# Linear attention on one core: how the rows of five output stores are cut into DMA transfers

## Chip, core and metric

The kernel runs on one core of a Trainium2 chip. The metric is the device time of one execution in microseconds (us); lower is better. Times are the median of several runs; 168.23 us is the median before (3 runs, 168.01 to 168.49).

## What is computed

Linear attention with an ELU feature map, for 32 heads, 2048 positions and 128 features, in bf16:

```python
B, H, S, D = 1, 32, 2048, 128          # q, k, v: bf16 [B, H, S, D]

def reference(q, k, v):
    phi_q = jnp.where(q > 0, q + 1, jnp.exp(q)) + 1e-6
    phi_k = jnp.where(k > 0, k + 1, jnp.exp(k)) + 1e-6
    kv = jnp.einsum("bhsd,bhse->bhde", phi_k, v)
    z = jnp.einsum("bhsd->bhd", phi_k)
    num = jnp.einsum("bhqd,bhde->bhqe", phi_q, kv)
    den = jnp.einsum("bhqd,bhd->bhq", phi_q, z)[..., None] + 1e-6
    return num / den
```

Each head reads three matrices of 512 KB and writes one.

## The kernel before

The work goes head by head, 32 in all. The 2048 positions of a head lie as 128 partitions of 16 positions each, so that one partition holds 16 x 128 bf16 values, a contiguous piece of 4 KB in DRAM. A load or a store of a whole head is therefore 128 rows of 4 KB.

For one head the steps are: ScalarE takes exp of k (line 368); VectorE clips it (line 382); GpSimd makes the positive part (line 372) and adds the two for some tiles (line 390); TensorE multiplies phi_k with v, and with a column of ones for z, into one PSUM bank (lines 413 and 320); ScalarE copies that to SBUF (line 430). TensorE transposes q into PSUM (line 436), ScalarE and VectorE make the parts of phi_q from it (lines 447, 454, 456, 468), and TensorE multiplies them with the copied state (lines 483 and 484). VectorE takes the denominators (506), their reciprocals (512), and divides into `o_sb` (517 and 524). For the last two heads ScalarE does some of the divisions (536).

k, q and v have 6 buffers each, the output has 10 (`NBO`): head h stores from buffer h % 10, and head h+10 may write there once that store has landed.

The order on each engine is written out by a small planner. Every operation is added with an engine and a number, its key; each engine runs its operations in the order of the keys, and the planner puts in the semaphore waits that follow from what operations read and write. All loads and stores are issued by the SP engine, one after the other: a load at line 361, with keys h - 7.95 (k), h - 6.9 (q) and h - 6.8 (v), and a store at line 571, with the key `late = h + 1.0 + 0.18 * h` (line 575). So stores fall further and further behind their heads: the loads of head 31 have keys of about 24, so the stores of heads 20 to 31 are all issued after the last load, in the order of the heads. Within a head's store the pieces have one key and are issued in the order in which they are added.

`PARTS` (line 252) says for which heads the store is cut, and into how many partitions each piece has; other heads are stored in one transfer of 128 partitions (lines 577 to 580). All pieces of a store count on the same semaphore. Head 31 is stored in two transfers of all 128 partitions, the first 9 of the 16 positions of each (rows of 2304 bytes) and the other 7 (1792 bytes); it isn't touched. Before, `PARTS` cuts head 29 alone.

Of the kernel before, what the change touches and what calls it, by code (L numbers as in the profile page):

```python
# [231 lines left out]
def bass_standalone__linear_attn_elu__prompt_kernel(  # L232
# [16 lines left out]
    NG = 7  # L249
    HALF = NT * P // 2  # L250
    LAST = NH - 1
    PARTS = {LAST - 2: (51, 13, 64)}

    ADD = (10, 11, 12, 13, 14)
    EVEN, ODD = tuple(range(0, NT, 2)), tuple(range(1, NT, 2))
# [9 lines left out]
    with ExitStack() as es:  # L265
# [85 lines left out]
        for h in range(NH):  # L351
# [218 lines left out]
            def store(t0, t1, key, parts, slot, p0=0, p1=P, h=h, bo=bo):  # L570
                pl.add("sp", key, lambda sp: sp.dma_start(rows(of, h)[p0:p1, t0 * D:t1 * D],
                                                          o_sb[p0:p1, bo, t0:t1].rearrange("p j d -> p (j d)")),
                       reads=[("o", bo, p) for p in parts], dma=("o", slot))

            late = h + 1.0 + 0.18 * h
            if h < LAST:
                p0 = 0
                for n in PARTS.get(h, (P,)):
                    store(0, NT, late, ("t", 0, 1, 2, 3, 4), bo, p0, p0 + n)
# [35 lines left out]
```

## Time and profile before

| | |
|---|---|
| median of 3 runs | 168.23 us (168.01 to 168.49) |
| the profiled execution | 167.82 us |
| its span, first to last instruction | 166.5 us |
| granted TensorE clock | 0.997 |
| busy: PE, DVE, ACT, POOL | 94%, 91%, 93%, 64% of the span |
| HBM read, written | 50.33 MB, 16.78 MB: 403 GB/s over the span |
| loads and whole stores, from issue to landing | 15.0 to 15.3 us |
| first store issued (line 571), last store issued | 20.9 us, 162.9 us |

The profile is one execution. "Busy" is an engine's time in instructions as a share of the span. A DMA transfer is split over the core's 16 DMA engines. The trace has a record for each packet that an engine moved (here a row of 4 KB, and a closing packet of 4 bytes that counts the semaphore up), with start and duration but without the number of the engine, and an event for each landing on a semaphore. The page lists the transfers of the stores by size; the whole ones are one line, the pieces of heads 29 and 31 have a line each:

```profile
out_dram<-o_sb SPq DMA_DIRECT2D x30, 512.0 KB, 15.3
out_dram<-o_sb SPq DMA_DIRECT2D x1, 288.0 KB, 3.7
out_dram<-o_sb SPq DMA_DIRECT2D x1, 256.0 KB
out_dram<-o_sb SPq DMA_DIRECT2D x1, 224.0 KB, 3.6
out_dram<-o_sb SPq DMA_DIRECT2D x1, 204.0 KB
out_dram<-o_sb SPq DMA_DIRECT2D x1, 52.0 KB
```

Columns are what is moved, the queue, the operation and its count, the size of one, and the median us from issue to landing where the trace has it: 51, 13 and 64 rows of 4 KB are 204, 52 and 256 KB.

### The profile page before, as it was taken

The numbers are of one execution on the slowest core, as the hardware profiler recorded it, in microseconds if no ns is written. First come the engines' busy times: TensorE is split into PE (matmuls) and PEld (weight loads), VectorE is DVE, ScalarE is ACT, GpSimd is POOL, SyncE is SP. The second block draws the span as 40 slices with busy tenths as digits, with TensorE's granted clock in tenths as the row PEclk, the third lists the DMA queues.
The fourth block names the chain that finished last, engine by engine and source line by source line (L and its number), as shares of the span: only waits on it lengthen the run. The fifth ranks groups of instructions, "written<-read, shape, count | busy, mean of one in ns | idle before, by whom it ended". The sixth has DMA issues, their size and how long they took to land.

```text
span 166.5 us, 6269 instructions
## 1 busy us (share of the span) xinstructions
PE 156.0 (94%) x2819; PEld 145.3 (87%) x2453; DVE 152.3 (91%) x270; ACT 155.0 (93%) x143; POOL 106.3 (64%) x128
## 2 busy tenths in 40 slices
PE   7789999999999999999999999999999999999960
PEld 0259999999999999899999989999998999999950
DVE  0587999999999999999999999999999999999991
ACT  3979999999999999999999999999999999998790
POOL 2405788676767877676778867676787767677300
PEclk9999999999999999999999999999999999999998
DMA  5999999999999999999999999999999999999986
GB/s 205 345 417 421 413 415 419 412 407 418 417 416 419 422 417 417 422 421 411 424 420 414 423 421 415 419 421 415 422 420 416 422 421 418 418 421 418 415 310 239
DMA packets 18605, 67.25 MB, mean 404 GB/s; under 512 B 2082, under 2 KB 2210, under 8 KB 18594
## 3 DMA queue, kind: packets, MB, share of 16 engines
q1 hardware_dynamic: 18592, 67.12, 99.4%
q8 instruction: 5, 0.08, 0.2%
q14 instruction: 6, 0.05, 0.1%
q10 hardware_dynamic: 2, 0.00, 0.0%
HBM read 50.33 MB, written 16.78 MB: 403 GB/s over the span
## 4 chain that ended last, share of the span: by engine, by line
DVE 58%; PE 17%; POOL 12%; ACT 6%; issue 3%; DMA 2%; DVEq 0%
DVE o_sb L524 20%; POOL rk_sb L390 12%; DVE rq_sb L456 11%; DVE emk_sb L382 10%; DVE emq_sb L468 9%; PE kvz_ps L413 6%; PE o_ps L483 5%; PE o_ps L484 5%; ACT ek_sb L368 3%; DVE rden_sb L512 3%; DVE o_sb L517 3%; ACT eq_sb L447 2%; DMA k_sb<-in_k_dram 2%; DVE den_sb L506 2%; DVE rk_sb L390 1%
## 5 line engine op out<-in xcount | busy, mean ns | idle before, releaser
L413 PE MATMUL kvz_ps<-v_sb,rk_sb 128*128 128x129 bf16 (+1 forms) x512 | 67.0, 220 | 2.8 <-DVE rk_sb L390 1.0
L524 DVE TENSOR_TENSOR o_sb<-o_ps,rden_sb 128x768 bf16<-128x768 f32 (+2 forms) x62 | 67.8, 1135 | 0.0
L390 POOL TENSOR_TENSOR rk_sb<-rk_sb,emk_sb 128x640 bf16<-128x640 bf16 x30 | 41.9, 1395 | 39.5 <-DVE emq_sb L468 38.2
L372 POOL TENSOR_SCALAR rk_sb<-k_sb 128x1024 bf16<-128x1024 bf16 (+1 forms) x60 | 64.1, 1068 | 2.5 <-DMA k_sb<-in_k_dram 2.5
L483 PE MATMUL o_ps<-kvs_sb,emq_sb 128*128 128x129 bf16 (+1 forms) x536 | 65.2, 217 | 0.0
L484 PE MATMUL o_ps<-kvs_sb,rq_sb 128*128 128x129 bf16 (+1 forms) x536 | 64.4, 217 | 0.0
L368 ACT ACTIVATE ek_sb<-k_sb 128x2048 bf16<-128x2048 bf16 x32 | 61.0, 1907 | 2.6 <-DMA k_sb<-in_k_dram 2.6
L447 ACT ACTIVATE eq_sb<-xT_ps 128x2048 bf16<-128x2048 bf16 (+1 forms) x33 | 60.0, 1821 | 2.0 <-PE xT_ps L436 2.0
L413 PE MATMUL kvz_ps<-v_sb,emk_sb 128*128 128x129 bf16 (+1 forms) x338 | 53.3, 221 | 0.6 <-DVE emk_sb L382 0.3
L413 PEld LDWEIGHTS kvz_ps<-v_sb,rk_sb 128*128 128x128 bf16 x512 | 46.1, 98 | 7.6 <-POOL rk_sb L390 2.7
L483 PEld LDWEIGHTS o_ps<-kvs_sb,emq_sb 128*128 128x128 bf16 x536 | 51.2, 98 | 0.8 <-issue 0.3
L484 PEld LDWEIGHTS o_ps<-kvs_sb,rq_sb 128*128 128x128 bf16 x536 | 51.3, 98 | 0.0
L436 PE MATMUL xT_ps<-ident,q_sb 128*128 128x128 bf16 x512 | 33.8, 219 | 0.6 <-DMA q_sb<-in_q_dram 0.4
L436 PEld LDWEIGHTS xT_ps<-ident,q_sb 128*128 128x128 bf16 x512 | 29.9, 98 | 5.1 <-DMA q_sb<-in_q_dram 4.2
L413 PEld LDWEIGHTS kvz_ps<-v_sb,emk_sb 128*128 128x128 bf16 x338 | 32.5, 98 | 0.9 <-DVE emk_sb L382 0.5
L320 PE MATMUL kvz_ps<-ones_sb,rk_sb 128*128 128x1 bf16 x232 | 31.3, 165 | 0.0
L454 ACT ACTIVATE rq_sb<-xT_ps 128x1024 bf16<-128x1024 bf16 x30 | 30.9, 1029 | 0.0
L382 DVE TENSOR_SCALAR emk_sb<-ek_sb 128x2048 bf16<-128x2048 bf16 x32 | 22.0, 688 | 5.6 <-ACT ek_sb L368 5.6
L456 DVE TENSOR_SCALAR rq_sb<-xT_ps 128x1024 bf16<-128x1024 bf16 x34 | 23.3, 690 | 1.1 <-PE o_ps L484 1.0
L468 DVE TENSOR_SCALAR emq_sb<-eq_sb 128x2048 bf16<-128x2048 bf16 x32 | 22.1, 690 | 0.0
L320 PE MATMUL kvz_ps<-ones_sb,emk_sb 128*128 128x1 bf16 x121 | 19.9, 166 | 0.0
L430 ACT ACTIVATE kvs_sb<-kvz_ps 128x129 bf16<-128x129 f32 x32 | 9.0, 281 | 1.6 <-PE kvz_ps L413 0.9
(28 smaller groups left out, 49.2 us busy)
## 6 DMA issues: line engine op xcount, KB each, us to landing
k_sb<-in_k_dram SPq DMA_DIRECT2D x32, 512.0 KB, 15.0
q_sb<-in_q_dram SPq DMA_DIRECT2D x32, 512.0 KB, 15.1
v_sb<-in_v_dram SPq DMA_DIRECT2D x32, 512.0 KB, 15.1
out_dram<-o_sb SPq DMA_DIRECT2D x30, 512.0 KB, 15.3
out_dram<-o_sb SPq DMA_DIRECT2D x1, 288.0 KB, 3.7
out_dram<-o_sb SPq DMA_DIRECT2D x1, 256.0 KB
out_dram<-o_sb SPq DMA_DIRECT2D x1, 224.0 KB, 3.6
out_dram<-o_sb SPq DMA_DIRECT2D x1, 204.0 KB
```

The costliest lines, as they stand in the source:

```text
L320: return pe.add_instruction(mybir.InstMatmult(start_tensor_calc=start, stop_tensor_calc=stop, ldweights=False, bass_skip_group_check=True, ...
L368: lambda a, bi=bi, b2=b2: a.activation(ek_sb[:, b2, :], k_sb[:, bi, :], ACT.Exp),
L372: pl.add(eng, key, lambda e: e.tensor_scalar(rk_sb[:, b3, c], k_sb[:, bi, c], BIG, 0.0, op0=ALU.min, op1=ALU.max), reads=[("k", bi)] + ([( ...
L382: lambda d, b2=b2, b3=b3: d.tensor_scalar(emk_sb[:, b3, :], ek_sb[:, b2, :], 1.0, EPS, op0=ALU.min, op1=ALU.add),
L390: return e.tensor_tensor(out=a, in0=a, in1=b, op=ALU.add)
L413: last = pe.matmul(kvz_ps[:, 1 - l:NC], lhsT=w, rhs=v_sb[:, bi, c - l:c + D], start=first, stop=fin, skip_group_check=True)
L436: last = pe.transpose(xT_ps[:, j * P:(j + 1) * P], q_sb[:, bi, j * P:(j + 1) * P], ident[:])
L447: halves[part] = pl.add("act", key, lambda a: a.activation(eq_sb[:, b2, c], xT_ps[:, c], ACT.Exp), reads=both[part:part + 1] or both, writ ...
L456: f = lambda d: d.tensor_scalar(rq_sb[:, b3, c], xT_ps[:, c], 0.0, None, op0=ALU.max)
L483: pe.matmul(o_ap, lhsT=emq_sb[:, b3, t * P:(t + 1) * P], rhs=kvs_sb[:, b3, c0:c1], start=True, stop=False)
L484: return pe.matmul(o_ap, lhsT=rq_sb[:, b3, t * P:(t + 1) * P], rhs=kvs_sb[:, b3, c0:c1], start=False, stop=True)
L524: pl.add("dve", key, lambda d: d.tensor_tensor(out=o_sb[:, bo, 3 * g0:3 * g1, :].rearrange("p (a b) d -> p a b d", b=3), in0=_ap(full, bas ...
```

## The change

Heads 6, 12, 18 and 24 are stored as five transfers each, of 112, 4, 4, 4 and 4 partitions, and head 29 in one transfer of 128. Everything else stays: the keys, the buffers, the order of the heads, the bytes that are moved in all.

```diff
@@ -249,7 +249,7 @@
     NG = 7
     HALF = NT * P // 2
     LAST = NH - 1
-    PARTS = {LAST - 2: (51, 13, 64)}
+    PARTS = {h: (112, 4, 4, 4, 4) for h in (6, 12, 18, 24)}
 
     ADD = (10, 11, 12, 13, 14)
     EVEN, ODD = tuple(range(0, NT, 2)), tuple(range(1, NT, 2))
```

## The prediction

> **What bounds the kernel now.** I read the page's slices and DMA rows first, then a table of stretches, then the waits, then the trace's single DMA records.
>
> ```profile
> DMA  5999999999999999999999999999999999999986
> GB/s 205 345 417 421 413 415 419 412 407 418 417 416 419 422 417 417 422 421 411 424 420 414 423 421 415 419 421 415 422 420 416 422 421 418 418 421 418 415 310 239
> ...
> q1 hardware_dynamic: 18592, 67.12, 99.4%
> ```
>
> One slice is 166.5 / 40 = 4.16 us. From the second slice to the last but two, the 16 DMA engines are full, at some 418 GB/s; only the last two slices (310, 239) are not. The stretches say the same about the end:
>
> ```profile
> core 0: us, PE busy (x) PEld busy (x) DVE busy (x) ACT busy (x) POOL busy (x), PEclk, DMA share, GB/s
> 60.00:140.00 80.00, 78.86 (x1480) 76.35 (x1293) 78.42 (x133) 79.02 (x68) 57.74 (x68) 1.00 1.03 419
> ...
> 162.00:164.00 2.00, 0.00 (x0) 0.00 (x0) 0.84 (x3) 0.73 (x3) 0.00 (x0) 1.00 0.99 380
> 164.00:165.00 1.00, 0.00 (x0) 0.00 (x0) 0.00 (x0) 0.00 (x0) 0.00 (x0) 1.00 0.70 276
> 165.00:166.50 1.50, 0.00 (x0) 0.00 (x0) 0.00 (x0) 0.00 (x0) 0.00 (x0) 0.69 0.17 66
> ```
>
> VectorE, ScalarE and TensorE are as full as the DMA engines until 158 us, but after 164 none of them works: only DMA engines do, and fewer and fewer of them (0.70, then 0.17). So the last 1.5 us belong to a few DMA engines that are behind. The waits show that loads are not what compute waits for:
>
> ```profile
> PEld xT_ps L436 <- DMA q_sb<-in_q_dram: 4.2, 1, 4.2
> ACT ek_sb L368 <- DMA k_sb<-in_k_dram: 2.6, 2, 1.5
> POOL rk_sb L372 <- DMA k_sb<-in_k_dram: 2.5, 1, 2.5
> PE xT_ps L436 <- DMA q_sb<-in_q_dram: 0.4, 1, 0.4
> ```
>
> These few are from the first heads. Later there is room: v of head 28 has landed at 138.01 while that head's transposes, which run ahead of its use, start at 139.83.
>
> **Which engines are behind.** A whole store leaves 16 landing events, one per engine. Head 28's, the last store that this change leaves alone, come at 159.06 plus 0.00 0.00 0.12 0.22 0.23 0.31 0.32 0.37 | 1.39 1.45 1.72 2.20 2.22 2.52 2.63 4.02 us. Eight engines are ahead, eight behind. The lags stay from transfer to transfer, since every engine always has work: nothing absorbs them. They grow where an engine fetches code (rows of 16 KB, 0.94 to 0.98 us each, at 16.2, 23.3, 30.7 and 37.6 us, after each of which one lag is about 1.45 larger), and on one engine, the last, by about 0.13 in every store, whose 4 KB packets take 178 to 182 ns there in place of 159.
>
> Head 29's three pieces tell who is who. They leave 3+1, 13+1 and 16 landings (the +1 are early, at 157.64 and 158.05, for the engines not used): 51 rows run on 3 engines (17 each), 13 on 13 (one each), 64 on 16 (four each). The two engines that run 17 rows after head 28 and can be followed from packet to packet are those with lags 1.39 and 1.45; the engine with 4.02 runs one row and then four, so it is in numbers 3 to 12. So are those with 1.72, 2.52 and one of 2.20 and 2.22; the other of that pair runs four rows only (13 to 15). 2.63 is most likely in 3 to 12 too, which makes five of these ten behind and five ahead.
>
> The Trainium skill, page DMA: Bandwidth & Descriptors, section "Why a DMA increments its semaphore by 16 and not by 1", says that a transfer runs on the largest number up to 16 that divides its partition count, on the lowest-numbered engines. The counts 3, 13 and 16 agree; that they are the lowest-numbered no run here shows, but I call the three engines 0 to 2.
>
> **Price of a row.** A 4 KB packet takes 159 ns and the next starts 3.5 ns before its end: 155.5 ns. The closing 4-byte packet takes 9, net 5.5. A whole transfer is 8 x 155.5 + 5.5 = 1.25 us per engine, as its ends show (1248 to 1249 ns apart).
>
> **The change part by part.**
>
> Removed: head 29's three pieces. Engines 0 to 2 had 17+1+4 = 22 rows there, 3 to 12 had 5, 13 to 15 had 4; now each has 8. That is 14 rows and 2 closings fewer on 0 to 2 (14 x 0.1555 + 0.01 = 2.19 us), 3 more on 3 to 12 (0.47), 4 more on 13 to 15 (0.62).
>
> Added: in each of heads 6, 12, 18 and 24, 112 rows are 7 per engine, and four pieces of 4 rows give, by the same reading, one row each to engines 0 to 3. Engines 0 to 3 get 3 rows and 4 closings more per head, in all 12 x 0.1555 + 16 x 0.0055 = 1.95 us; 4 to 15 get 4 rows fewer (0.62).
>
> So a handicap at head 29's end is the lag of head 28 plus what the pieces add. Before: engines 0 and 1 have 1.39 and 1.45 + 2.19 = 3.58 and 3.64; the last one 4.02 - 0.47 = 3.55. These three are the ones that end the span: their packets go on without a gap through heads 30 and 31 (1.25 + 0.72 + 0.57 us) to the last landing at 166.48. After: 3.34 and 3.40 for 0 and 1, 4.02 - 0.62 = 3.40 for the last. Alone that is 3.64 - 3.40 = 0.24 us less.
>
> Engine 3 decides. It had 3 rows fewer and now has 12 more. If it is one of the five ahead, it ends at 0.37 + 1.95 = 2.32: harmless. If it is behind: 1.72 gives 3.67 (+0.03 against 3.64), 2.20 gives 4.15 (+0.51), 2.52 gives 4.47 (+0.83), 2.63 gives 4.58 (+0.94), 4.02 gives 5.97 (+2.33). The trace names no engine number. Its neighbours speak for behind: of 0 to 2 two of three are, of 13 to 15 one of three. I take the middle of the four that cost, +0.88 us.
>
> Hidden: SP issues 16 transfers more and 2 fewer. An issue at L571 takes 0.315 to 1.05 us when it isn't held up, so four more are 1.3 to 4.2 us of SP's time per head, and the k, q and v loads behind them on its queue wait so long. Cover: loads take 15.0 us from issue to landing, so the engines have more than ten us of queue. Without that cover it would be up to 4.2 us per head.
>
> Hidden too: the loads on engines 0 to 3 land later, by 0.98 us after head 12's store (6 rows, 8 closings) and 1.47 after head 18's, against 1.8 us or more of room (138.01 to 139.83, and 150.66 to 153.98 for head 31's v). Their waits take the place of nothing.
>
> Unknown: what a 4-row transfer costs beyond its row. Lower end 0 (the 13-row piece took 161 ns per busy engine, row and closing); upper end 0.28 us, as the first rows after an idle engine took 300 to 440 ns, so 16 x 0.28 = 4.5 us. I take 0, since these engines are never idle; that is the row it is nearest to. A saving is unknown as well: 28 rows of the slow engine in stores of 112 rows could run at 159 in place of 179 (0 to 0.56 us less).
>
> The Trainium skill, same page, section "Latency and other measured facts", says that DMA engines 7 and 15 are usually slower, and ties that to a kind of transfer not used here. Were the slow engine 7, engine 3 would not be it, and the +2.33 would fall out: the sum would then be the middle of three, +0.83. No run here shows its number.
>
> **Sum.** The profiled execution took 167.82, 1.3 around its span of 166.5. 167.82 + 0.88 = 168.70; the median of the runs is 0.41 above that execution, so 169.1.
>
> **Rivals.**
> - Engine 3 is ahead (or the 1.72 one): -0.24 to +0.03, so 168.0 to 168.3. For it: five of ten are ahead. Against it: its neighbours.
> - Faster: rows lie on engines otherwise than I read. If the 4-row pieces hit engines that are ahead and the slow engine's 28 rows in 112-row stores run at 159 ns, the handicaps are 0.83 on 0 and 1 and 4.02 - 0.62 - 0.56 = 2.84 on the slow one: 0.80 less, 167.4. It decides once no engine is above 3.1. Against it: the 3 and 13 fit the divisor reading.
> - The change doesn't do what it says: 4 rows are spread so that nobody gets more. Then 4.02 is left uncorrected, +0.38: 168.6. The 13-row piece on 13 engines speaks against it.
> - Small transfers cost a slow first row: 1 to 4.5 us more on engines 0 to 3, 169 to 172.7. Only idle engines show such rows.
>
> **Chances.** Forecast 0.51, engine 3 ahead 0.25, faster 0.15, spread 0.05, slow small rows 0.04. No change is within 0.3%, 0.5 us, about what can be told here. Slower: 0.51 + 0.04 + 0.01 of spread = 0.56. Same: 0.25 + 0.04 = 0.29. Faster: 0.15. The likeliest case alone reaches from +0.5 to +2.33, 168.7 to 170.6. Over all I give 167.6 to 170.6, which leaves out most of the faster case and the slow rows.
>
> **What would show it.** Right: each 4-row piece leaves 4 landings and one early one; one engine's lag grows by about 0.49 in each of the four cut stores from a start of 2 or more; head 28's largest lag is above 4.1; and after 165 us a single engine works on. Wrong: head 28's largest lag at 3.4 and a span of 166.2 to 166.5 (engine 3 ahead), 4-row pieces that leave other than 4 landings, or compute waiting for k, q or v after head 4.

## The result and the profile after

| | before | after |
|---|---|---|
| median (7 runs each) | 168.05 us (167.84 to 168.49) | 169.28 us (168.53 to 170.25) |
| ratio to before | 1 | 1.0076, 95% interval 1.0053 to 1.0099 |
| the profiled execution | 167.82 us | 170.25 us |
| its span | 166.5 us | 169.0 us |

The change makes the kernel slower, by 1.23 us in the medians. The profiled execution of after is the slowest of its seven runs, so its 2.43 us over that of before are more than the usual loss.

The page of after, its rows of slices and of DMA queues (one slice is 169.0 / 40 = 4.22 us):

```profile
DMA  5999999999999999999999999999999999999961
GB/s 198 350 416 421 415 415 419 414 422 413 417 419 420 419 417 420 415 420 420 421 419 419 419 421 416 420 418 419 421 419 419 418 422 420 418 420 415 379 279 69
...
q1 hardware_dynamic: 18640, 67.12, 98.0%
q8 instruction: 5, 0.08, 0.2%
q14 instruction: 6, 0.05, 0.1%
```

The middle is what it was, some 419 GB/s. The loss lies in the last slices: 69 GB/s in the last one, where before still had 239. The 48 packets more on q1 (18640 against 18592) are closing packets, 64 more in the four cut heads and 16 fewer in head 29; they cost no bandwidth that can be seen. Stretches of after, with the DMA share and GB/s in the last two columns:

```profile
core 0: us, PE busy (x) PEld busy (x) DVE busy (x) ACT busy (x) POOL busy (x), PEclk, DMA share, GB/s
60.00:140.00 80.00, 78.86 (x1479) 76.34 (x1290) 78.45 (x133) 79.04 (x69) 58.04 (x68) 1.00 1.03 419
...
162.00:164.00 2.00, 0.00 (x0) 0.00 (x0) 1.12 (x4) 0.98 (x4) 0.00 (x0) 1.00 0.97 388
164.00:165.00 1.00, 0.00 (x0) 0.00 (x0) 0.00 (x0) 0.00 (x0) 0.00 (x0) 1.00 0.62 244
165.00:166.50 1.50, 0.00 (x0) 0.00 (x0) 0.00 (x0) 0.00 (x0) 0.00 (x0) 0.57 0.23 91
166.50:169.00 2.50, 0.00 (x0) 0.00 (x0) 0.00 (x0) 0.00 (x0) 0.00 (x0) 0.50 0.05 20
```

Between 60 and 140 us all is equal to before. From 166.5 us on, where before had ended, 0.05 of 16 engines work: 0.8 of an engine, so one engine alone moves the last 2.5 us. Compute has no part in it, and the loads that now land later are not waited for; the waits of after list the same four as before, within 0.2 us:

```profile
PEld xT_ps L436 <- DMA q_sb<-in_q_dram: 4.3, 1, 4.3
...
ACT ek_sb L368 <- DMA k_sb<-in_k_dram: 2.8, 2, 1.6
...
POOL rk_sb L372 <- DMA k_sb<-in_k_dram: 2.6, 1, 2.6
...
PE xT_ps L436 <- DMA q_sb<-in_q_dram: 0.5, 1, 0.5
```

The landings of head 28's store in after, the first at 158.62 us, and then the lag of each engine behind it:

```
0.00 0.04 0.05 0.08 0.17 0.18 | 1.03 1.46 1.51 1.55 2.30 2.55 3.00 3.20 4.00 6.60
```

The engine that loses 0.13 us per store has its 4.00, as before (4.02). The other one, 6.60, is new, and it ends the kernel: head 31's last transfer has its first landing at 165.53, fifteen engines have landed by 166.43, and the last one lands at 168.92. In what follows this engine is called L.

### The profile page after: what moved, and what is told of

The parts are those of the page before. It is cut to its first block, busy times and chain, and to the rows that moved or that the text cites. A ratio compares the mean times of both kernels' runs of the same rounds, so it can differ in the third digit from the quotient of the medians.

```text
span 169.0 us, 6283 instructions
## 1 busy us (share of the span) xinstructions
PE 156.1 (92%) x2819; PEld 145.3 (86%) x2453; DVE 152.5 (90%) x270; ACT 155.2 (92%) x143; POOL 106.4 (63%) x128
## 3 DMA queue, kind: packets, MB, share of 16 engines
q1 hardware_dynamic: 18640, 67.12, 98.0%
## 4 chain that ended last, share of the span: by engine, by line
DVE 60%; PE 16%; POOL 12%; DMA 4%; issue 3%; ACT 1%; SPq 1%; DVEq 0%
DVE o_sb L524 21%; POOL rk_sb L390 12%; DVE rq_sb L456 11%; DVE emq_sb L468 10%; DVE emk_sb L382 10%; PE kvz_ps L413 5%; PE o_ps L483 5%; PE o_ps L484 5%; DMA k_sb<-in_k_dram 4%; DVE rden_sb L512 3%; DVE o_sb L517 3%; DVE den_sb L506 2%; ACT ek_sb L368 1%; SPq L361 1%; DVE rk_sb L390 0%
```

## Experiments

Every kernel is the one before with `PARTS` (line 252) changed, unless the diff shows more. e1 to e4 share one set of runs of before (median 168.08 us), e5 to e8 a second (167.96), e9 and e10 a third (167.91), e11 and e12 a fourth (167.95).

**e1_whole: no store is cut.**

```diff
-    PARTS = {LAST - 2: (51, 13, 64)}
+    PARTS = {}
```

> No store is cut but head 31's. Theory (an engine that is behind sets the end): the handicap of the slow engine stays at 4.02 and that of the engine with 2.63, which may also serve the code fetch near 158.5 us, at 2.63 to 4.08, against 3.64 before: 0.4 us slower than before, ratio 1.002 to 1.004, and 0.6 to 1.0 us faster than the changed kernel. Rival (small transfers or their issue cost the time): nothing small is left, so not slower than before, 1.000 or below.

Measured: 168.29 us, ratio 1.0008 (0.9986 to 1.0030). In head 28's store the largest lags are 2.43, 2.77 and 4.12: without a cut, the slow engine is last. The ratio expected was 1.002 to 1.004; the measured one can't be told from 1. Leaving the cut of head 29 out costs at most 0.3% of the time, 0.5 us; it isn't what costs 1.2 us, the four new cuts are.

**e2_three: which engines a piece runs on.**

```diff
-    PARTS = {LAST - 2: (51, 13, 64)}
+    PARTS = {h: (112, 3, 3, 3, 7) for h in (6, 12, 18, 24)}
```

> Heads 6, 12, 18 and 24 as 112, 3, 3, 3 and 7 partitions: five transfers each as in the changed kernel, with the same 11 rows on engines 0 to 2, but 8 in place of 11 on engine 3, and 8 in place of 7 on engines 4 to 6. Theory (engine 3 is the one that is late): 12 rows, 1.9 us, come off it, so the end is set by others at handicaps of 3.4 to 4.1: 168.0 to 168.5, ratio 1.000 to 1.003. Rival (small transfers or issue cost): as the changed kernel, 1.007. Second rival (the late one is among 0 to 2): as the changed kernel, 1.007.

Measured: 168.23 us, ratio 1.0008 (0.9990 to 1.0026). Across head 24's cut three lags grow by 0.65 us (1.96, 2.37, 2.52 to 2.61, 3.03, 3.15), three by 0.16 (2.06, 2.10, 2.15 to 2.20, 2.26, 2.32), and the slow engine's from 3.82 to 4.27, that is by its own 0.13 for each of two stores and 0.19 more. Three rows on each of three engines and one on four others is what pieces of 3 and 7 give when each runs on as many engines as it has rows, and the 3 are not among the other four. L, known here by its jump at 104 us (0.89 to 1.84, see e5), gains 0.16 in a cut, and at least 0.6 in every cut of after. So it is among the four engines of a 4-row piece, but not among the three of a 3-row piece: by the prediction's numbering it is engine 3. The slow engine is one of the next three (4 to 6).

**e3_even: five transfers, but the same rows on every engine.**

```diff
-    PARTS = {LAST - 2: (51, 13, 64)}
+    PARTS = {h: (64, 16, 16, 16, 16) for h in (6, 12, 18, 24)}
```

> Heads 6, 12, 18 and 24 as 64 and four times 16 partitions: five transfers each, all on 16 engines, so every engine has its 8 rows. Theory (imbalance): as with no cut at all, 0.4 us slower than before, 1.002 to 1.004. Rival (small transfers or issue cost): as the changed kernel or slower, 1.007 or more, since the four 16-partition pieces burden all 16 engines.

Measured: 168.46 us, ratio 1.0012 (0.9996 to 1.0027), span 167.1. Cutting four heads into five transfers each costs some 0.4 us at most (0.38 by the medians, 0.45 by the upper end of the interval). With e2, which also has five transfers a head, it shows that the number of transfers isn't what costs: the uneven rows do, where they fall on L.

**e4_who: pieces of n and 16 - n rows.**

```diff
-    PARTS = {LAST - 2: (51, 13, 64)}
+    PARTS = {h: (h - 7, 23 - h, 112) for h in range(8, 16)}
```

> Heads 8 to 15 as n, 16 - n and 112 partitions with n = 1 to 8, which gives engine j one row more for j < n and one more for j < 16 - n: a number for each lag in the landings. Theory: the engine with number 3 has a lag of 1.7 or more before head 8's store, and two of 0, 1 and 2 have less than that. Rival: engine 3 is one of the eight that are ahead. It also shows if 0 to n - 1 are the engines of a transfer of n rows: each cut should move the lags of n engines by 0.16 us. The time means little; 168 to 170.

Measured: one run of 169.15 us. Each of the eight cut stores leaves 34 landings, (n + 1) + (16 - n + 1) + 16, so each count up to 15 runs on just as many engines. A number for each of the 16 lags couldn't be had from it: several engines run within 0.1 us of each other and change places. For the numbering it is inconclusive.

The Trainium skill, page DMA: Bandwidth & Descriptors, section "Why a DMA increments its semaphore by 16 and not by 1", has the rule that these counts follow, the largest divisor up to 16, on the lowest-numbered engines. The runs bear out the count (34 landings here, 36 in a cut store of after), and that smaller sets lie within larger ones; the numbers themselves no record shows.

**e5_again: after, a second time**, with nothing changed from it.

> The changed kernel once more, for a second profile. Theory (engine 3, with a lag of about 1.7 of its own, gets 2.6 more than its neighbours by the four cuts; what code fetches add on top, 1.0 near 103.8 us and 1.45 near 158 us, may fall on another engine from run to run): 168.5 to 170.3, median near 169.2; in this profile the lag of the last engine at head 28 is 4.2 to 6.7, and it is one of four that gain 0.65 in every cut. Rival (the fetches always fall on engine 3): again 6.6, with the same two jumps, at 170.2 in the profile.

Measured: 169.92 us, ratio 1.0101 (1.0046 to 1.0157). The profile (170.41 us, span 169.1) has L at 6.90 in head 28's store. The rival expected here came, and not the theory: in both profiles of after the same lag has three jumps, beside those of the cuts: 1.12 to 2.06 and 1.40 to 2.37 at 42 us, 2.51 to 3.57 and 2.92 to 3.93 at 104 us, and, in head 27's landings, 5.85 to 6.70 and 6.15 to 6.98. At 42, 104 and 162.8 us the trace has a packet of 8192 bytes on q14, a code fetch, of 309 ns each; the next two rows take 381 to 487 ns at the first two and 301 and 367 at the last, in place of 159. The packets of L can be followed in this trace, since each starts 3 to 4 ns before the one ahead of it ends. From the end of head 24's 112 rows (start in us, bytes, ns):

```
157.88 4096 293 | 158.17 4096 458 | 158.63 4 9
158.63 4096 159 | 158.79 4 9 | 158.79 4096 159 | 158.95 4 9
158.95 4096 159 | 159.11 4 9 | 159.12 4096 159 | 159.27 4 9
159.28 4096 159 ... 160.36 4096 159 | 160.52 4 9      (head 25, 8 rows)
160.53 4096 159 ... 161.61 4096 159 | 161.77 4 9      (head 26, 8 rows)
161.77 4096 159 ... 162.71 4096 159                   (head 27, 7 rows)
162.86 8192 309 | 163.17 4096 367 | 163.53 4096 301
```

Four times one row and a closing: this engine has the 4-row pieces. Then the fetch, on the same engine. (Where several engines run in step a link could be to a neighbour's packet; L's landings fit, 0.34 to 0.47 us behind each closing.) The first line is another loss, for which see e11.

**e6_two: only two of the four heads.**

```diff
-    PARTS = {LAST - 2: (51, 13, 64)}
+    PARTS = {h: (112, 4, 4, 4, 4) for h in (6, 12)}
```

> 112, 4, 4, 4, 4 for heads 6 and 12 alone: half of the rows. Theory (the end is the later of the slow engine and engine 3): engine 3 is at about 1.7 + 1.3 = 3.0 against 4.0 of the slow one, so as with no cut at all, 168.0 to 168.5, ratio 1.000 to 1.003. Rival (each cut store costs the same): half of the loss, 168.7, ratio 1.0035 to 1.004.

Measured: 168.21 us, ratio 1.0013 (0.9976 to 1.0050). Two of the four cuts give 0.25 us by the medians, where four give 1.2 to 2.0. But the interval holds the theory's 1.000 to 1.003 and the rival's half loss alike, so whether the loss is linear in the cuts stays open here. The runs go from 167.79 to 170.14: eight are at 168.39 or below, four at 169.34 or above. The profiled execution is one of the four (169.38 us); there L has 4.74 in head 27's store, 5.57 in head 28's, against the slow engine's 4.28. So in that execution L ends the kernel, with far more than the 3.0 of the theory.

**e7_eight: eight heads.**

```diff
-    PARTS = {LAST - 2: (51, 13, 64)}
+    PARTS = {h: (112, 4, 4, 4, 4) for h in (6, 9, 12, 15, 18, 20, 22, 24)}
```

> 112, 4, 4, 4, 4 for eight heads (6, 9, 12, 15, 18, 20, 22, 24): twice the rows. Theory (engine 3 and its three neighbours set the end): 12 rows and 16 closings more on them, 1.95 us, so the changed kernel's time plus 1.95, with four fewer on the others, 171.0 to 171.5, ratio 1.017 to 1.021. Rival (each cut store costs the same): twice the loss over no cut, 168.3 + 2.0 = 170.3, ratio 1.013.

Measured: 172.83 us, ratio 1.0289 (1.0241 to 1.0337). Four more cuts cost 2.9 us over e5 and 3.55 over the first run of after, where 4 x 0.49 = 1.95 was worked out: the direction holds, the size is missed. Compute waits for loads as before, in the same four places (4.2, 2.5, 1.8 and 0.4 us), so late loads aren't the reason. In the page the late engines now show as two last slices at under half of the bandwidth (199 and 33 GB/s):

```profile
DMA  5999999999999999999999999999999999999850
GB/s 205 390 422 414 421 414 421 372 416 411 426 415 422 418 418 419 418 421 416 424 416 423 418 422 415 417 422 418 422 416 425 416 423 418 419 403 372 323 199 33
```

Bandwidth falls from the slice at 150 us on (403, 372, 323), where before had 418 until 158. From 150 to 158.3 us, 31 rows of 4 KB take 250 to 809 ns; after has two of them there, in a stall that e11 and e12 look into. They go with the excess of 1.0 to 1.6 us; what makes them is open.

**e8_late: the split of head 29 with one engine more.**

```diff
-    PARTS = {LAST - 2: (51, 13, 64)}
+    PARTS = {LAST - 2: (52, 12, 64)}
```

> Head 29 alone as 52, 12 and 64 partitions: 18 rows on engines 0 to 3, 5 on 4 to 11, 4 on 12 to 15, so engine 3 gets 10 rows more than in a whole store, 13 more than before, and 0 to 2 get 4 fewer than before. Theory (engine 3 is behind): with its lag of 1.7 to 2.7 and 10 rows it is at 3.3 to 4.3, against 3.64 before: 167.8 to 168.8, ratio 0.998 to 1.004. Rival (it is the place, early and four times, and not engine 3 that costs): as before, 1.000 or below.

Measured: 168.55 us, ratio 1.0031 (1.0005 to 1.0057), span 167.2. The expectation had the split wrong. Fifty-two rows run on 13 engines, 4 each, and not on four with 13 each: the store leaves 43 landings, (13 + 1) + (12 + 1) + 16. So twelve engines have 9 rows in place of a whole store's 8, and this kernel doesn't load L alone and can't test what it was made for. What it does is to take the slow engine's relief away, which had 5 rows before. It is last: its lag of 4.12 in head 28's store and one row more make 4.28, 0.64 over the 3.64 that ended before, and the span is 0.7 longer. So the cut of 51, 13 and 64 was of some use beside this one, as it took rows off that engine; beside no cut at all (e1) its use can't be told.

**e9_nofetch and e10_control: without the third code fetch.** VectorE's division of the last tile (line 517) is left out for heads 10 to 25, so the last 128 positions of these heads are not computed. e9 has the `PARTS` of after, e10 those of before.

```diff
-                last_tile(h + 0.92)
+                if not 10 <= h < 26:
+                    last_tile(h + 0.92)
```

> The changed kernel, with the division of the last tile (line 517) left out for heads 10 to 25; of those heads the last 128 of the 2048 positions are not computed, and what lay in the buffer is stored. VectorE has 16 instructions fewer. Theory (late fetch): the code fetch of six or so 8-KB rows' worth that came at about 162.7 us in the changed kernel belongs to VectorE and is counted by its instructions, so with 16 fewer it comes later than VectorE's work lasts, and isn't there. The late engine's lag then doesn't grow by about 0.8 us after head 27's landing: span about 168.2, time 168.3 to 168.8, some 0.8 us under the changed kernel's 169.3 to 169.9; the fetch near 104 comes some us later than before. Rival 1 (another engine's fetch, or one by the clock): a fetch near 162 stays, and the time with it, 169.3 to 169.9. Rival 2 (the fetch goes, but costs nothing at the end): no packet near 162, time still 169.3 to 169.9.

> The kernel before, with the same division of the last tile left out for heads 10 to 25 (the same positions are not computed). Theory: the late fetch falls there on an engine that has some 0.5 us of room, so its going gives nothing: 167.7 to 168.2 beside 168.0, span 166.2 to 166.6. Rival (leaving work out speeds the kernel up by itself): both this and the changed kernel gain the same, 0.5 us or more.

Measured: e9 169.18 us, ratio 1.0083 (1.0059 to 1.0108); e10 168.16 us, ratio 1.0024 (1.0007 to 1.0042). The page of e9, its length and its queues of code:

```profile
span 167.1 us, 6267 instructions
...
q8 instruction: 5, 0.08, 0.2%
q14 instruction: 5, 0.04, 0.1%
```

Sixteen instructions fewer (after has 6283), and one fetch fewer: the one near 162 us is gone, and the one near 104 comes at 108.3. In e10 it is the same (108.5, and none near 162). So these two fetches are VectorE's, and they come by its count of instructions. In e9's trace no lag jumps after head 25's store: L has 4.72 from head 25 to head 29, where after went from 5.85 to 6.70. But the time expected didn't come. The median lies 0.10 us under the first run of after and 0.74 under the second, and by the ratio (1.0083) e9 lies between the two (1.0076 and 1.0101); 168.3 to 168.8 was expected. Only the profiled execution (168.61), the fastest of the six, is there, and in it L had a better start (a lag of about 0.8 us ahead of head 6's cut, against 1.9 in after). So the fetch is shown in the lag, and its price in the time is not shown. e10 shows that leaving the work out gives nothing by itself; it is even 0.07 to 0.42% slower than before, for which no reason is known.

**e11_21 and e12_3: another head in place of 24.** In after's, e5's and e9's traces L gained 0.60 to 0.67 us in the cuts of heads 6, 12 and 18 where it can be followed, but 1.23, 1.07 and 1.28 in that of head 24: the last rows of its 112-row piece took 325 and 522 ns, 293 and 458 (the first line of the list above), and 796. That is 0.43 to 0.64 us more than those rows should.

```diff
-    PARTS = {LAST - 2: (51, 13, 64)}
+    PARTS = {h: (112, 4, 4, 4, 4) for h in (6, 12, 18, 21)}
```

```diff
-    PARTS = {LAST - 2: (51, 13, 64)}
+    PARTS = {h: (112, 4, 4, 4, 4) for h in (3, 6, 12, 18)}
```

> The changed kernel with the fourth cut store moved from head 24 to head 21: the same rows on every engine. In the changed kernel's three traces the late engine gained 0.65 us more than the whole-row engines' neighbours in the cuts of heads 6, 12 and 18, but 1.07 to 1.28 in that of head 24, where the last rows of the 112-row piece took 293 to 796 ns in place of 159. Theory (late cut): that comes with a cut that is moved after the last loads have landed (147 us); head 21's store is moved at 150 to 154, so it has it too, and the time stays at 169.0 to 169.9. Rival (a stall that belongs to about 157 us, by the clock): head 21 gains 0.65 alone; an extra 0.4 to 0.6 us is then seen in another store at 157, or, if it takes a cut to show it, not at all, 168.6 to 169.2.

> The changed kernel with heads 3, 6, 12 and 18 cut in place of 6, 12, 18 and 24, all before the last loads have landed; the same rows on every engine. Theory (late cut): each cut adds 0.65 us to the late engine, none more; no row of 293 to 796 ns near 157 us; its lag in head 28's store 5.4 to 6.2 rather than 6.6 to 6.9, time 168.6 to 169.2, some 0.5 us under the changed kernel. Rival (the lag itself brings the stall, wherever the last cut is): a cut or whole store late in the run shows the extra 0.4 to 0.6 us all the same, 169.2 to 169.9.

Measured: e11 168.88 us, ratio 1.0057 (1.0034 to 1.0081); e12 168.58 us, ratio 1.0032 (1.0010 to 1.0053). Neither trace has such a row near 157 us. In e11 L goes from 3.66 to 4.26 in head 21's cut, +0.60, though that store is moved after the last loads: the theory of a late cut falls in that form. In e12 L is at 5.15 from head 18's cut to head 26's store; then the fetch takes it to 6.16. So the stall doesn't come with a lag of a given size either: e9's cut of head 24 has it at 3.44, e12's cut of head 18 hasn't at 4.50. In these traces it comes with the cut of head 24, on L alone. The rival, a stall that belongs to some 157 us and takes a cut to show it, isn't excluded: in e7 the largest lag grows by 1.23 us, and not 0.65, in the cut of head 22 already (5.75 to 6.98), and with such a lag that engine moves its rows of this store between 155 and 158 us. What makes those rows slow stays open. The rows per engine are the same in e11, e12 and after, and by the medians 168.88 and 168.58 are 0.4 to 1.3 us less than 169.28 and 169.92. But the interval of e11 (1.0034 to 1.0081) overlaps that of after (1.0053 to 1.0099), and that of e12 ends where after's begins. So a gain by moving the cut of head 24 isn't shown for e11 and only likely for e12. The stretches of e12's end show L alone again, for a shorter time than in after:

```profile
core 0: us, PE busy (x) PEld busy (x) DVE busy (x) ACT busy (x) POOL busy (x), PEclk, DMA share, GB/s
...
164.00:165.00 1.00, 0.00 (x0) 0.00 (x0) 0.00 (x0) 0.00 (x0) 0.00 (x0) 1.00 0.81 312
165.00:166.50 1.50, 0.00 (x0) 0.00 (x0) 0.00 (x0) 0.00 (x0) 0.00 (x0) 0.85 0.10 41
166.50:169.00 2.50, 0.00 (x0) 0.00 (x0) 0.00 (x0) 0.00 (x0) 0.00 (x0) 0.50 0.03 12
```

No version beats the one before: e1, e2, e3 and e6 can't be told from it, e4 has a single run, and the others are slower.

## Why the prediction was right, point by point

- **The bound** (the end is set by the DMA engine that is furthest behind): right. After 164 us no engine but DMA works, and one engine is alone for the last 2.5 us.
- **The relief of the two 17-row engines and of the slow one** (-0.24 us by itself): it can't be seen, since L is later by more. In after none of the three is last; in e1, without any cut, the slow engine is, and in e8, too.
- **Four cuts put 3 rows and 4 closings more on each of four engines**: right. Each cut leaves 36 landings, 16 + 4 x (4 + 1). Four lags grow by 0.65 us in a cut (head 24: 1.93, 2.36, 2.57 to 2.58, 3.02, 3.22, and L, with the stall on top). The prediction gave 0.49; that counts from a store of 8 rows, and the engines ahead, from which the lag is taken, have only 7 in a cut store. 4 rows and 4 closings are 4 x 0.1555 + 4 x 0.0055 = 0.644.
- **Engine 3 is among those behind**: right. By its jumps (in before 0.92 to 1.88 at 42 us and 1.79 to 2.75 at 104) it is the one with 2.63 in head 28's store of before, one of the four prices listed (+0.94), next to the middle that was taken (+0.88). That it was behind was a guess from its neighbours, at little more than even odds, and that the middle of four prices lay beside the right one was luck.
- **The size**: +0.88 was too little; the medians have +1.23 (first run of after) and +1.96 (e5), the profiles of before and after +2.43. That 169.1 lies within 0.2 us of 169.28 is luck in part: the median before that it was added to, 168.23, came out as 168.05 with more runs, and e5 has 169.92. The step that failed is the lag of engine 3, which was carried unchanged from head 28 of before to the end. By rows alone it would have come to 2.63 + 4 x 0.65 = 5.23 in head 28's store. The trace has 6.60. What was left out is the third code fetch, 0.85 us, and the stall of head 24's cut, 1.23 - 0.65 = 0.58; 5.23 + 0.85 + 0.58 = 6.66. The same two terms on the +0.94 of this engine give 2.37, beside the +2.43 of the profiles. (It fits this well because L's lag ahead of the first cut is much the same in both profiles, 1.8 and 1.9 us; in e5 it is 2.3.) The profile of after is the slowest of its runs; how much of each term the others had, and so what makes up the +1.23, no run shows. In before the same fetch, at 162.0 us, cost nothing, as the engine had room: about 2.63 - 0.47 + 0.8 = 2.96 against the 3.64 that ended it. In after it falls on the path. The list of code fetches in the prediction had only the 16 KB rows of the first 40 us; the trace of before has this one, too.
- **Small transfers cost nothing** (0 taken, 4.5 us the upper bound): right, by e3. L's pieces start 0.161 us apart, row and closing. The reason given, that only idle engines show slow rows, was wrong: behind the fetch at 103.5 us of before an engine with a full queue has rows of 405 and 487 ns.
- **Later loads hidden, SP's 16 issues hidden**: right, by the waits.
- **The slow engine**: right in that it ends no later (4.00 against 4.02). The saving held possible, faster rows in stores of 112, isn't seen: its lag grows by 0.26 us over the stores of heads 24 and 25 (3.40 to 3.66), as over two whole ones. The Trainium skill, page DMA: Bandwidth & Descriptors, section "Latency and other measured facts", names 7 and 15 as usually slower; e2 puts the slow one among the seven engines of a 7-row piece and outside the three of a 3-row piece, so by the lowest-numbered reading, in which L is 3, it is one of 4 to 6 and neither of the page's two. That is no contradiction, as the page ties its finding to a kind of transfer not used here.
- **What would show it**: pieces of four landings and head 28's largest lag above 4.1 (6.60) came. The lag that ends the kernel grows in each cut, but so do three others, it starts at 1.9 and not above 2, and the growth per cut was given too small by the row just named. A single engine is at work only from 166.43 us on (0.05 of 16), and not from 165 (0.23 of 16 until 166.5).

## What to carry to other kernels

When the DMA queues are full to the end, as here, the end of the kernel belongs to the DMA engine that is furthest behind, and cutting a transfer into pieces of few partitions gives rows to the same few engines each time: count rows per engine, not transfers. Before adding rows to an engine, read from the landings of a whole transfer which engines are behind, and then which fetches or slow rows are still to come on just that engine; a delay that was harmless while the engine had room is added to its lag at the end once it is last (0.85 us here). Two such cuts cost nothing that could be told, four cost 0.3 to 1.0%, by which heads and in which set of runs, and eight 2.9%.

## What the runs showed of the hardware

- The code fetches at 42, 104 and 162 us all fall on one DMA engine in after, e5 and e11, and each costs it 0.8 to 1.05 us (309 ns for the packet, most of the rest in the two rows behind it). The last two are VectorE's, as e9 and e10 show. With a full queue that time isn't made good: in before the lag is 2.75 behind the fetch at 104 us and still 2.63 at 159.
- The lags with which the engines leave the first microseconds differ from run to run: L's, ahead of head 6's cut, was 1.9 us in after, 2.3 in e5, 2.6 in the profiled execution of e6, 1.1 in e11 and 0.8 in e9. Whether that makes the spread of the times isn't shown, as a run without a profile shows no lags. The runs of after spread over 1.7 and 2.5 us (e5), those of before over 0.7 and 2.2 beside them.
- Rows of 290 to 800 ns in place of 159 appear on L in the cut of head 24 (after, e5, e9) and, but for rows behind a code fetch, nowhere in the cuts of heads 3, 6, 12, 18 and 21; with eight cuts there are 31 of 250 ns and more between 150 and 158.3 us. The cause stays open.
